# Two blocks of x turned by VectorE instead of TensorE in the projection stage of a fused attention and SwiGLU kernel

## The chip, the cores and the metric

The kernel runs on one core of a Trainium2 chip. The metric is the device time of one execution in microseconds (us); less is better. Three runs of the kernel before the change took 1405.27, 1405.49 and 1405.62 us, with a median of 1405.49 us.

## The reference

The input `x` has 2048 tokens of 512 features. It is layer-normalised, and the normalised `xn` goes two ways: into 32-head attention with heads of 16 features, and into a SwiGLU feed-forward of width 1792. The output is `x` plus the product of the two.

```python
def _A_ref(x, wqkv, wo):            # H = 32 heads, Dh = 16
    q, k, v = split(x @ wqkv)
    p = softmax(q @ k.T * Dh ** -0.5)
    return merge(p @ v) @ wo

def _B_ref(x, w_gate, w_up, w_down):
    return (silu(x @ w_gate) * (x @ w_up)) @ w_down

xn = _layernorm(x)
return x + _A_ref(xn, wqkv, wo) * silu(_B_ref(xn, w_gate, w_up, w_down))
```

## The kernel before

**Two stages.** The first stage, about 160 us of 1403 us, normalises `x`, turns it so that features lie on partitions, and makes q, k and v. They go to DRAM, together with the turned `x` (`xt_d`). The second stage runs attention and feeds the matmuls of the feed-forward into the same TensorE queue. The change touches the first stage only.

**Blocks and tiles.** The tokens are cut into NB = 4 blocks of TB = 512, and a block into NT = 4 pieces of 128 tokens. The loop `for b in range(NB)` makes twelve result tiles a block: in blocks 1 to 3 the tiles n = 0 to 7 are `feature_tile` (q and k, 128 features by 512 tokens) and n = 8 to 11 are `value_tile` (v, 128 tokens by 512 features). Every tile is one call of `project`: 12 matmuls, since each of the 4 slices of 128 features takes three products. Both the turned `x` and the weights are held as a high and a low part (`hi`, `lo`), and the products are high by high, low by high, high by low, in this order.

**What follows a tile.** After a feature tile ScalarE squares the result (`sq`, L701), casts it to the high part (`parts`, L702), VectorE subtracts to get the low part (L703), and the SP queue stores both (L705). After a value tile ScalarE copies it into `vt` (L719). The result banks `ps` are four. In block 0 and in the tiles 0 to 6 of block 1 ScalarE also copies a piece of the turned `x` of block 0 into `fx` (`copy_fx`, L732). At the end of tile 8 `flush(b)` puts the eight sums of squares on TensorE (`squares`, L663), each of which needs its `sq`, and VectorE takes two maxima (L743).

**How the next block is made.** While block b is projected, block b + 1 is prepared: the SP queue loads four pieces of `x` into `xin`, the tile `facc` under another name (`load_x`, L544); VectorE takes mean and variance of a piece (`stats`, L610 and L611); `rates` gets the inverse deviations, with a square root on ScalarE (L615 to L623); VectorE normalises (`norm`, L627); TensorE turns a piece by four transposes with an identity into a PSUM bank (`turn`, L631); and `split_x` makes the two parts, the high one by ScalarE (L636), the low one by VectorE (L639). After the last piece the POOL queue stores both parts (L645). The schedule by tile n is written out by hand:

```python
if n == (1 if b else 2) and more:
    load_x(b + 1)
...
if 2 <= n < 6:  stats(n - 2)
if n == 5:      rates(0, NT)
if 6 <= n < 10: norm(n - 6)
if 8 <= n < 11: turn_x(b + 1, n - 8)
if n == 10:     turn_x(b + 1, NT - 1)
```

The queues are in order: an instruction that waits holds up all behind it on its engine. The first matmul of the next block needs the high part of its first 128 features, and the second matmul the low part.

Of the kernel before, what the change touches and what calls it, by code (L numbers as in the profile page):

```python
# [9 lines left out]
F32 = mybir.dt.float32  # L10
# [3 lines left out]
AF = mybir.ActivationFunctionType  # L14
ALU = mybir.AluOpType
# [4 lines left out]
P = 128  # L20
# [6 lines left out]
TB = S // NB  # L27
NT = TB // P
DT = D // P
# [13 lines left out]
PROBS = 12  # L43
EPS = 1e-5
FINE = (30,)
QSLOT = (0, 1, 0)
KSLOT = (0, 0, 1)

# [2 lines left out]
def tile_block(ctx: ExitStack, tc: tile.TileContext, x, wqkv, wo, w_gate, w_up, w_down, out):  # L51
    nc = tc.nc
    ctx.enter_context(tc.manual_schedule())
    x, out = x[0], out[0]
    mm, act, dve, sp, pool = nc.tensor.matmul, nc.scalar.activation, nc.vector, nc.sync, nc.gpsimd
# [6 lines left out]
    xt_d = dram.tile([NB, 2, P, DT, TB], F32, name="xt_d")  # L62
# [31 lines left out]
    def load_rows(dst, src, slots):  # L94
        for h in range(2):
            for s, part in enumerate(slots):
                r = h * HALF + 2 + s * DH
                sp.dma_start(dst[r:r + DH].bitcast(F32),
                             src[part].rearrange("(j h d) t -> h d j t", j=2, h=2)[h])
# [5 lines left out]
    def load_q(u, i=None):  # L105
        g, b = divmod(u, NB)
        load_rows(qst[u % 2 if i is None else i], q_d[:, g * 64:(g + 1) * 64, b * TB:(b + 1) * TB], QSLOT)

# [382 lines left out]
    for u in range(units):  # L491
# [3 lines left out]
        elif u == 0:  # L495
            ns = [4, 6, 6]
        elif u in FINE:
            ns = [4] * 4
# [32 lines left out]
    with ExitStack() as pro:  # L531
        pc = pro.enter_context(tc.tile_pool(name="pc", bufs=1))
# [8 lines left out]
        xin = facc  # L541

        def load_tile(t):
            sp.dma_start(xin[:, t % NT], x[t * P:(t + 1) * P])  # L544

        def load_x(b):
            for t in range(NT):
                load_tile(b * NT + t)
# [50 lines left out]
        for t in range(NT):  # L599
            dve.memset(vt5[:, :, t, :, DH:], 1.0)  # L600
        xt = [[pc.tile([P, DT, TB], F32R, name=f"xt{i}{j}") for j in range(2)] for i in range(2)]
        mv = pc.tile([P, NT, dve.BN_AGGR_DIM], F32, name="mv")
        ve = pc.tile([P, NT], F32, name="ve")
        rs = pc.tile([P, NT], F32, name="rs")
        nw = pc.tile([P, NT], F32, name="nw")
# [2 lines left out]
        def stats(t):  # L608
            st = p2.tile([P, dve.BN_STATS_DIM], F32, tag="st", name="st")
            dve.bn_stats(st, xin[:, t])  # L610
            dve.bn_aggr(mv[:, t], st)  # L611

        def rates(first, last):
            r, n, v = (i[:, first:last] for i in (rs, nw, ve))
            dve.tensor_scalar(v, mv[:, first:last, 1], EPS, None, op0=ALU.add)  # L615
            act(n, v, AF.Sqrt)
            dve.reciprocal(r, n)
            each = [[i[:, t:t + 1] for i in (rs, nw, ve)] for t in range(first, last)]
            for rt, n1, vt1 in each:
                dve.tensor_scalar(n1, vt1, rt, rt, op0=ALU.mult, op1=ALU.mult)  # L620
            dve.tensor_scalar(n, n, -0.5, 1.5, op0=ALU.mult, op1=ALU.add)
            for rt, n1, _ in each:
                dve.tensor_scalar(rt, n1, rt, None, op0=ALU.mult)  # L623
# [10 lines left out]
        def split_x(b, t, av, between=None):  # L634
            hi, lo = (xt[b % 2][j][:, :, t * P:(t + 1) * P] for j in range(2))
            nc.scalar.copy(hi, av)  # L636
            if between:
                between()
            dve.tensor_sub(lo, av, hi.bitcast(F32))  # L639

        def turn_x(b, t, between=None):
            split_x(b, t, turn(t), between)
            if t == NT - 1 and b:
                for j in range(2):
                    pool.dma_start(xt_d[b, j], xt[b % 2][j].bitcast(F32))  # L645


        def project(pairs, xh, xl, tokens, order=None, ps=None):
# [21 lines left out]
        part = split_w(8, pool)  # L670
# [6 lines left out]
        part = split_w(10, pool)  # L677
# [67 lines left out]
        for b in range(NB):  # L745
            more = b + 1 < NB
            slots = [(feature_tile, m) for m in range(8)]
            slots = [(value_tile, t) for t in range(NT)] + slots if b == 0 else slots + [(value_tile, t) for t in range(NT)]
            for n, (make, i) in enumerate(slots):
                if b == 0:  # L750
                    if n + 5 < 12:
                        load_w(worder[n + 5])
                    if n >= 2 and n + 2 < 12:
                        split_w(worder[n + 2], pool)
                if n == (1 if b else 2) and more:
                    load_x(b + 1)
                if b == 2 and n in (6, 7):
                    load_gu(n - 6)
                if b == 2 and n == 8:
                    load_wd(0)  # L760
                if not more and n == 2:
                    split_gu(0)
                    tidy()
                    for bank in acc:
                        dve.memset(bank, 0.0)
                if not more and n in (1, 3):
                    load_k(0, n // 2)
                if not more and n == 5:
                    load_q(0)
                if not more and n == 6:  # L770
                    for c in range(2):
                        load_v(0, c)
                if b == 0 and n == 1:
                    rates(2, NT)
                    norm(2)
                    norm(3)
                    split_x(0, 0, xf)
                made = make(b, i)
                if b == 0 and n == 1:
                    for t in (2, 3):  # L780
                        turn_x(0, t)
                if b < 2 and 0 <= 12 * b + n - 3 < 16:
                    copy_fx(12 * b + n - 3)
                if n == 0 and b == 1:
                    flush(0)
                if make is feature_tile:
                    pend.append(made)
                if b == 0 and n == 11:
                    ring(0, 2, one)
                    queries(0, one)  # L790
                if more:
                    if 2 <= n < 6:
                        stats(n - 2)
                    if n == 5:
                        rates(0, NT)
                    if 6 <= n < 10:
                        norm(n - 6)
                    if 8 <= n < 11:
                        turn_x(b + 1, n - 8)
                    if n == 10:  # L800
                        turn_x(b + 1, NT - 1)
                if n == 8 and b:
                    flush(b)
                if not more and n == 8:
                    dve.reduce_max(pk, peak, axis=AX.X)
                    dve.tensor_add(sm, pk[:, 0:1], pk[:, 1:2])
                if not more and n == 9:
                    tops = pps.tile([P, 512], F32, tag="ps", name="tops")
                    nc.tensor.transpose(tops[0:1, :P], sm, ident)
                    dve.reduce_max(s4, tops[0:1, :P], axis=AX.X)  # L810
                    dve.tensor_scalar(s4, s4, 0.51, None, op0=ALU.mult)
                    dve.tensor_scalar(flag, s4, LIMIT, None, op0=ALU.is_le)
                    dve.tensor_scalar(sel[:, :NG * NB], row[:, :NG * NB], s4, None, op0=ALU.mult)
                    for h in range(2):
                        dve.tensor_copy(selq[:, h * HALF:h * HALF + 1], s4)
                    fill(3 * DC)
                    tidy()
                    low, high = [pps.tile([P, 512], F32, tag="ps", name="low") for _ in range(2)]
                    mm(high[:2 * NG * NB, :8], sel, row[:, :8], start=True, stop=True, skip_group_check=True)
                    mm(low[:HALF + 2, :8], selq, row[:, :8], start=True, stop=True, skip_group_check=True)  # L820
                    act(shift, high[:2 * NG * NB, 0:1].to_broadcast([2 * NG * NB, 512]), AF.Copy, scale=-1.0)
                    for h in range(2):
                        two_rows = slice(h * HALF, h * HALF + 2)
                        act(qst[0][two_rows], low[two_rows, None, 0:1].to_broadcast([2, 2, 512]), AF.Copy, scale=-1.0)
                    for j in range(4):
                        pool.dma_start(sh_d[:, j * 512:(j + 1) * 512], shift.bitcast(F32))
                    fast = nc.values_load(flag, min_val=0, max_val=1)


        with tc.If(fast < 1):  # L830
            with tc.tile_pool(name="gen", bufs=1) as gen:
                for h in range(2):
                    pool.memset(qst[0][h * HALF:h * HALF + 2].bitcast(F32), 0.0)
                for g in range(NG):
                    for b in range(NB):
# [3 lines left out]
                        for j in range(NB):  # L839
                            load_k(g, j, j % 2)  # L840
                            for i in range(4 * NT):
                                h, t = divmod(i, NT)
# [132 lines left out]
    for now, (u, first, n) in enumerate(blocks):  # L975
        g, b = divmod(u, NB)
# [25 lines left out]
    hi = two.tile([P, 2, D], F32R, tag="guh", name="rh")[:, 0]  # L1002
    lo = one.tile([P, D], F32R, tag="th", name="rl")
# [38 lines left out]
    part = low(1)  # L1042
# [35 lines left out]
```

## Time and profile before

| | before |
|---|---|
| median of 3 runs | 1405.49 us |
| the profiled execution | 1405.18 us |
| its span on the core | 1403.4 us |
| TensorE (PE) busy | 1395.8 us, 99% |
| ScalarE (ACT) busy | 1082.7 us, 77% |
| VectorE (DVE) busy | 753.5 us, 54% |
| GpSimd (POOL) busy | 90.6 us, 6% |
| granted TensorE clock, mean | 0.999 |

The profile is one execution. A row of the timeline gives the start in us from the start of the span, the duration, the engine, the line of the kernel, the operation, and in brackets the idle time of the engine ahead of it with what ended it. Instructions of one engine overlap at their ends, so that what counts in a queue is the distance from start to start. Tiles of the projection can be told by their `sq` (L701) and `vt` (L719) rows: one of these starts as each tile of TensorE ends.

### The profile page before, as it was taken

The page shows a single profiled execution, that of the slowest core. Times are in us where ns is not written, and L with a number is a line of the kernel's source. Part 1 is how long each engine was busy: PE and PEld are TensorE (multiplying, and loading weights), DVE is VectorE, ACT ScalarE, POOL GpSimd, SP SyncE. Part 2 cuts the span into 40 slices and gives each one's busy share as a digit, 9 for nine tenths or more (in the row PEclk, how much of TensorE's full clock was granted, in tenths as well). Part 3 has the DMA queues.
Part 4 walks back from the last instruction along what each step waited for, and adds up shares of the span by engine and source line. Part 5 has one row for each costly group of instructions (what it writes and reads, how often), then busy time and mean ns, then how long its engine had stood idle before and what let it go on. Part 6 is the DMA issues. An engine that isn't in the chain of part 4 may idle for free.

```text
span 1403.4 us, 27734 instructions
## 1 busy us (share of the span) xinstructions
PE 1395.8 (99%) x11227; PEld 847.1 (60%) x11227; DVE 753.5 (54%) x1291; ACT 1082.7 (77%) x1235; POOL 90.6 (6%) x104
## 2 busy tenths in 40 slices
PE   9999999999999999999999999999999999999998
PEld 7777756556555655565556556655655565565554
DVE  5544455345645553555456645654565446556655
ACT  6733587778788877887887788778877887888885
POOL 4200200000000000000000000000000000000333
PEclk9999999999999999999999999999999999999999
DMA  6768651033544521144524303256224113224333
GB/s 219 263 248 247 181 128 43 13 103 88 122 102 103 125 50 35 47 118 107 131 64 104 101 13 73 73 143 145 65 73 109 37 46 73 66 89 162 102 99 113
DMA packets 126956, 148.17 MB, mean 106 GB/s; under 512 B 12524, under 2 KB 79340, under 8 KB 126052
## 3 DMA queue, kind: packets, MB, share of 16 engines
q1 hardware_dynamic: 121620, 125.79, 34.2%
q0 software_dynamic: 4912, 20.12, 3.9%
q8 instruction: 91, 1.49, 0.4%
q14 instruction: 45, 0.37, 0.1%
q10 hardware_dynamic: 288, 0.39, 0.1%
HBM read 106.68 MB, written 39.58 MB: 104 GB/s over the span
## 4 chain that ended last, share of the span: by engine, by line
PE 88%; ACT 0%; DVE 0%; issue 0%; DVEq 0%; ACTq 0%
PE acc L406 32%; PE bankx L186 24%; PE score L888 17%; PE banky L186 12%; PE acc L888 3%; PE acc L1015 0%; PE banky L1015 0%; ACT pr L961 0%; ACT pr L894 0%; PE score L1015 0%; DVE y L1022 0%; DVE fx L280 0%; DVE part L300 0%; DVE y L191 0%; DVE pr L947 0%
## 5 line engine op out<-in xcount | busy, mean ns | idle before, releaser
L894 ACT ACTIVATE pr<-score 128x1024 f32<-128x1024 f32 x856 | 810.6, 1032 | 229.3 <-PE score L888 227.8
L406 PE MATMUL acc<-pr,vst 128*17 128x512 f32 x4096 | 461.9, 593 | 0.0
L888 PE MATMUL score<-qst,kst 50*128 50x512 f32 x1712 | 392.0, 413 | 0.0
L186 PE MATMUL bankx<-fx,guh 64*128 64x512 f32 x896 | 333.4, 393 | 0.1
L186 PE MATMUL banky<-fx,guh 64*128 64x512 f32 x896 | 324.5, 392 | 0.0
L406 PEld LDWEIGHTS acc<-pr,vst 128*17 128x17 f32 x4096 | 108.8, 97 | 286.4 <-issue 262.6
L888 PEld LDWEIGHTS score<-qst,kst 50*128 50x128 f32 x1712 | 176.0, 184 | 147.7 <-issue 67.2
L947 DVE COPY pr<-acc 128x512 f32<-128x512 f32 x168 | 116.2, 691 | 192.5 <-PE acc L888 187.0
L186 PE MATMUL bankx<-wd,hh 64*128 64x512 f32 x672 | 200.2, 392 | 0.0
L186 PE MATMUL banky<-wd,hh 64*128 64x512 f32 x672 | 197.8, 393 | 0.0
L186 PEld LDWEIGHTS bankx<-fx,guh 64*128 64x128 f32 x896 | 166.4, 186 | 18.0 <-issue 0.9
L186 PE MATMUL bankx<-fx,gul 64*128 64x512 f32 x448 | 175.4, 391 | 0.0
L186 PE MATMUL banky<-fx,gul 64*128 64x512 f32 x448 | 175.4, 391 | 0.0
L961 ACT ACTIVATE pr<-pr 128x1024 f32<-128x1024 f32 x168 | 172.5, 1079 | 0.0
L186 PEld LDWEIGHTS banky<-fx,guh 64*128 64x128 f32 x896 | 166.3, 186 | 6.1
L953 DVE COPY pr<-acc 128x512 f32<-128x512 f32 x168 | 116.2, 692 | 73.8 <-PE acc L888 60.3
L888 PE MATMUL acc<-qst,kst 50*128 50x512 f32 x336 | 135.4, 403 | 0.1
L239 DVE SCALAR_TENSOR_TENSOR ga<-th,bankx 128x512 f32<-128x512 f32 x56 | 38.5, 688 | 178.2 <-ACT th L238 178.2
L186 PEld LDWEIGHTS bankx<-wd,hh 64*128 64x128 f32 x672 | 124.9, 186 | 12.4
L186 PEld LDWEIGHTS banky<-wd,hh 64*128 64x128 f32 x672 | 124.4, 186 | 3.6
L186 PEld LDWEIGHTS bankx<-fx,gul 64*128 64x128 f32 x448 | 83.7, 187 | 10.3
L186 PEld LDWEIGHTS banky<-fx,gul 64*128 64x128 f32 x448 | 83.5, 186 | 3.6
(168 smaller groups left out, 1308.7 us busy)
## 6 DMA issues: line engine op xcount, KB each, us to landing
gur<-in_B_w_gate_dram SPq DMA_DIRECT2D x56, 256.0 KB
gur<-in_B_w_up_dram SPq DMA_DIRECT2D x56, 256.0 KB
wdr<-in_B_w_down_dram SPq DMA_DIRECT2D x56, 256.0 KB
kst<-k_d SPq DMA_DIRECT2D x192, 64.0 KB
qst<-q_d SPq DMA_DIRECT2D x192, 64.0 KB
fx<-xt_d SPq DMA_DIRECT2D x24, 512.0 KB
q_d<-parts SPq DMA_DIRECT2D x16, 512.0 KB
k_d<-parts SPq DMA_DIRECT2D x16, 512.0 KB
```

What stands on the lines that cost most here:

```text
L186: mm(banks[i], lhs[halves[i]], rhs[halves[i]], start=start, stop=stop)
L239: dve.scalar_tensor_tensor(ga, th, 1.0, bankx, op0=ALU.add, op1=ALU.mult)
L406: mm(acc[0][h * 32:h * 32 + DH + 1], v[:, kt % CT, h * (DH + 1):(h + 1) * (DH + 1)], probs[kt, h // 2][:, h % 2], start=kt == 0, stop=kt = ...
L888: mm(bank, k[r, j, kc * P:(kc + 1) * P], qst[u % 2][r, j], start=True, stop=True)
L894: act(pr, score[slot], AF.Exp, scale=0.25)
L947: dve.tensor_copy(probs[kt, j][:, 0], spare_bank)
L953: dve.tensor_copy(probs[kt, j][:, 1], spare_bank)
L961: act(probs[kt, j], probs[kt, j], AF.Exp, scale=0.25)
```

## The change

It concerns the preparation of the blocks 2 and 3, which runs during the blocks 1 and 2; block 1 is prepared during block 0 as before. The load is issued at tile 0 instead of tile 1. All statistics are taken at the tiles 2 and 3, and `rates` at tile 3. ScalarE normalises in place, by `Identity` with a scale and an offset for each partition (`norms`, at the tiles 3 and 4). Then VectorE turns the block by 16 transposes, each of 32 partitions by 512 elements, which writes 32 partitions of another tile, `xw`, in general in another quadrant (`turn_quarter`, from tile 5 on: 2, 2, 3, 3, 3, 3). Behind tile 10 `split_block` makes the parts, one 128-feature slice after the other: four ScalarE copies and four VectorE subtractions, and then the two stores. The 16 transposes of TensorE, the four `norm` of VectorE and the four `split_x` of each of these two blocks go away.

```diff
+TURNS = (0, 0, 0, 0, 0, 0, 2, 4, 7, 10, 13, 16, 16)
...
+        xw = pc.tile([P, DT, TB], F32, name="xw")
+        off = pc.tile([P, NT], F32, name="off")
...
             if t == NT - 1 and b:
-                for j in range(2):
-                    pool.dma_start(xt_d[b, j], xt[b % 2][j].bitcast(F32))
+                store_x(b)
+
+        def store_x(b):
+            for j in range(2):
+                pool.dma_start(xt_d[b, j], xt[b % 2][j].bitcast(F32))
+
+        def norms(first):
+            if first == 0:
+                dve.scalar_tensor_tensor(off, mv[:, :, 0], -1.0, rs, op0=ALU.mult, op1=ALU.mult)
+            for t in range(first, first + 2):
+                act(xin[:, t], xin[:, t], AF.Identity, scale=rs[:, t:t + 1], bias=off[:, t:t + 1])
+
+        quarter = [slice(i * 32, (i + 1) * 32) for i in range(4)]
+
+        def turn_quarter(i):
+            q, g = divmod(i, 4)
+            dve.transpose(xw[quarter[q]].rearrange("p c (t g l) -> p g t c l", g=4, l=32)[:, g],
+                          xin[quarter[g]].rearrange("p t (c q d) -> p q t c d", q=4, d=32)[:, q])
+
+        def split_block(b):
+            hi, lo = xt[b % 2]
+            for c in range(DT):
+                nc.scalar.copy(hi[:, c], xw[:, c])
+                dve.tensor_sub(lo[:, c], xw[:, c], hi[:, c].bitcast(F32))
+            store_x(b)
...
-                if n == (1 if b else 2) and more:
+                if n == (0 if b else 2) and more:
                     load_x(b + 1)
+                if more and b:
+                    for part in range(TURNS[n], TURNS[n + 1]):
+                        turn_quarter(part)
...
-                if more:
+                if more and b:
+                    if n in (2, 3):
+                        stats(2 * n - 4)
+                        stats(2 * n - 3)
+                    if n == 3:
+                        rates(0, NT)
+                    if n in (3, 4):
+                        norms(2 * n - 6)
+                    if n == 10:
+                        split_block(b + 1)
+                elif more:
                     if 2 <= n < 6:
                         stats(n - 2)
```

## The prediction

> **What bounds the kernel now.** I read the page's busy shares first, then the chain of work that ended last, then the first stage row by row.
>
> ```profile
> PE 1395.8 (99%) x11227; PEld 847.1 (60%) x11227; DVE 753.5 (54%) x1291; ACT 1082.7 (77%) x1235; POOL 90.6 (6%) x104
> PE 88%; ACT 0%; DVE 0%; issue 0%; DVEq 0%; ACTq 0%
> 82.00:84.00 2.00, 2.00 (x11) 1.61 (x10) 0.00 (x0) 0.59 (x1) 0.53 (x1) 1.00 0.79 328
> ```
>
> These are a line of the page's busy times, one of its chain, and a row of a table by stretches. TensorE (PE) is the chain, and the third row (a stretch across the border between blocks 1 and 2: PE, PEld, DVE, ACT and POOL busy, clock, DMA share, GB/s) shows it busy and at full clock there, with VectorE idle and ScalarE nearly so. So a TensorE instruction removed here is worth its time, if the next block's parts still come in time. What TensorE gives to the turns is read from the timeline, from the distances between the ends of tiles in blocks 1 and 2.
>
> ```profile
> 49.24 0.60 ACT L701 ACTIVATE sq<-ps 128x512 bf16<-128x512 f32 x1 [0.66 <-PE ps L656]
> 52.78 0.60 ACT L701 ACTIVATE sq<-ps 128x512 bf16<-128x512 f32 x1 [1.53 <-PE ps L656]
> 55.58 0.60 ACT L701 ACTIVATE sq<-ps 128x512 bf16<-128x512 f32 x1 [0.65 <-PE ps L656]
> ...
> 72.38 0.59 ACT L719 COPY vt<-ps 128x512 f32<-128x512 f32 x1 [1.72 <-PE ps L658]
> 83.22 0.59 ACT L719 COPY vt<-ps 128x512 f32<-128x512 f32 x1 [2.09 <-PE ps L658]
> ...
> 108.41 0.59 ACT L719 COPY vt<-ps 128x512 f32<-128x512 f32 x1 [1.72 <-PE ps L658]
> 119.26 0.59 ACT L719 COPY vt<-ps 128x512 f32<-128x512 f32 x1 [2.09 <-PE ps L658]
> ...
> 79.38 1.04 PE L631 MATMUL acc<-ident,xn 128*128 128x128 f32 x8
> ```
>
> A tile takes 55.58 − 52.78 = 2.80. With the eight sums of squares between, it takes 52.78 − 49.24 = 3.54, so these cost 0.74. From tile 8's end to tile 11's end lie three tiles, one set of squares and all 16 transposes: 83.22 − 72.38 = 10.84, less 3 × 2.80, less 0.74, leaves **1.70** for the transposes of block 1. Block 2 gives 10.85, so 1.71. Removed for good: **3.4 us**, 0.24% of the time. That is the most that the change can give.
>
> **What is put in its place, and when it ends.** Before, the pieces were normalised, turned and split one by one, so little was left at the end. Now the next block's first matmul needs ScalarE's copy of `xw`, which needs all 16 turns, and these need all four normalisations. That is one chain; it is added up from its start at tile 3.
>
> ```profile
> 58.38 0.60 ACT L701 ACTIVATE sq<-ps 128x512 bf16<-128x512 f32 x1 [0.79 <-PE ps L656]
> 58.88 0.58 ACT L702 CAST parts<-ps 128x512 fp32r<-128x512 f32 x1
> 59.48 1.05 ACT L732 CAST fx<-xt 64x1024 fp32r<-64x1024 f32 x1
> ...
> 59.49 0.69 DVE L703 TENSOR_TENSOR parts<-ps,parts 128x512 fp32r<-128x512 f32 x1 [0.85 <-ACT parts L702]
> 60.10 0.69 DVE L610 BATCH_NORM_STATS2 st<-facc 128x6 f32<-128x512 f32 x1
> 60.82 0.18 DVE L611 BATCH_NORM_AGGREGATE mv<-st 128x2 f32<-128x6 f32 x1
> 66.42 0.18 DVE L611 BATCH_NORM_AGGREGATE mv<-st 128x2 f32<-128x6 f32 x1
> 66.63 0.17 DVE L615 TENSOR_SCALAR ve<-mv 128x4 f32<-128x4 f32 x1
> 68.35 0.58 DVE L623 TENSOR_SCALAR rs<-nw,rs 128x1 f32<-128x1 f32 x4
> 95.49 0.18 DVE L611 BATCH_NORM_AGGREGATE mv<-st 128x2 f32<-128x6 f32 x1
> 95.59 0.67 DVE L703 TENSOR_TENSOR parts<-ps,parts 128x512 fp32r<-128x512 f32 x1
> ```
>
> *Statistics.* In block 1 tile 3's subtraction stands at 59.49 and two pieces follow: 0.61 to the first `stats`, 0.72 to its aggregate, 0.10 on, 0.72 again, 0.21 to `ve` at 61.85. From `ve` to the end of `rs` the trace shows 68.35 + 0.58 − 66.63 = 2.30, ScalarE's square root within it; `off` adds one small operation, 0.2 by the 0.17 of `ve`. So the factors are ready at 64.35. ScalarE's `norms` stand at the head of its queue and hold tile 4's `sq` (due at 58.38 + 2.80 = 61.2) behind them.
>
> ```profile
> 30.35 0.60 ACT L574 CAST wh<-wraw 128x512 fp32r<-128x512 f32 x1
> 30.86 0.59 ACT L701 ACTIVATE sq<-ps 128x512 bf16<-128x512 f32 x1
> L620 DVE TENSOR_SCALAR nw<-ve,rs 128x1 f32<-128x1 f32 x16 | 3.5, 268 | 0.2
> L615 DVE TENSOR_SCALAR ve<-mv 128x1 f32<-128x1 f32 x2 | 0.3, 154 | 0.1
> ```
>
> *Normalisations.* No row shows an `Identity` with a scale and an offset for each partition. The nearest are a ScalarE cast from SBUF, 0.60 long and 0.51 to the next, and on VectorE the price of two such operands, 268 − 154 ns = 0.11. I take 0.63 from start to start and 0.71 long; the ends are 0.51 and twice the surcharge, 0.74. The Trainium skill (ScalarE: Activation LUTs, What ACT_TABLE_LOAD costs) gives about 93 ns for each such operand of an activation. By that page the two would cost 0.19, an estimate, and the sum would be 0.6 higher; no run here shows it. In block 1: norms at 64.40 and 65.03; `sq` at 65.66, cast 66.16, `fx` copy 66.76; norms at 67.84 and 68.47, done at **69.2**. In block 2 there is no `fx` copy: on the old clock the cast of tile 3 (94.91, 0.58 long) lets the subtraction start at 95.52, so `ve` stands at 97.88, the factors at 100.38, norms at 100.43 and 101.06, `sq` 101.69, cast 102.19, norms at 102.79 and 103.42, done at **104.15**.
>
> ```profile
> 356.14 0.71 DVE L442 STREAM_TRANSPOSE o<-on 128x512 f32<-128x512 f32 x1
> 356.79 0.69 DVE L953 COPY pr<-acc 128x512 f32<-128x512 f32 x1
> ...
> 94.91 0.58 ACT L702 CAST parts<-ps 128x512 fp32r<-128x512 f32 x1
> L574 ACT CAST wh<-wraw 128x512 fp32r<-128x512 f32 x8 | 5.0, 620 | 0.1
> L417 DVE STREAM_TRANSPOSE o<-acc 128x512 f32<-128x512 f32 x31 | 22.2, 717 | 37.6 <-PE acc L406 37.6
> L426 DVE TENSOR_TENSOR on<-o,rl 128x256 f32<-128x256 f32 x31 | 12.9, 417 | 0.1
> 82.80 0.39 PE L658 MATMUL ps<-vl,xt 128*128 128x512 f32 x1
> 83.03 0.62 PE L656 MATMUL ps<-xt,wh 128*128 128x512 f32 x2
> 119.06 0.62 PE L656 MATMUL ps<-xt,wh 128*128 128x512 f32 x2
> ```
>
> *Turns.* These are rows of the timeline and of the groups by line. No row shows a turn of 32 partitions into another quadrant. The dense turn of as many elements per partition takes 0.71 and lets the next start after **0.65**; I take that, since the elements in each lane decide in all rows of this kind. Below, the bound is 0.61, the ordinary distance (59.49 to 60.10); above, 0.75, a turn from PSUM (717 ns) whose follower waits for its end. Sixteen turns are 10.4, and three subtractions and two maxima stand between them in VectorE's queue, 5 × 0.61 = 3.05: their own inputs come in time (tile 5's cast ends at 70.2, the subtraction's turn comes at 70.5). The last turn ends 0.05 after its distance: 69.2 + 13.5 = **82.7** and 104.15 + 13.5 = **117.65**. Then the copy 0.62 + 0.03 and the subtraction 0.69 + 0.03, as at the handovers in the rows: the second matmul of the next block at **84.1** and **119.05**.
>
> *Against before.* Its second matmul stood 0.62 − 0.39 = 0.23 behind the first, at 83.26 and 119.29. Block 1 is therefore 0.8 longer, block 2 0.2 shorter; the later slices follow at 0.6 each, faster than TensorE eats them (0.7 for three). Without a wait the matmuls would come 1.7 earlier, so TensorE stands 2.5 in block 1 and 1.5 in block 2. Sum: **+0.6**.
>
> *The rest is covered.* The eighth square of block 1 needs `sq` of tile 7. Behind the norms ScalarE still has tiles 5 and 6, with `sq`, cast and `fx` copy 2.2 each, so that this `sq` ends at 69.1 + 4.4 + 0.6 = 74.1. Tile 8 ends at 72.4 as before, and the squares would be through by 73.1; TensorE waits about 1.0, but the border's wait gets shorter by as much: it is part of the 2.5. Result banks come free in time: tile 9's needs the subtraction of tile 5, done at 71.2, and is wanted at 74. Not used any more on VectorE and ScalarE, `norm` and `split_x` lay beside matmuls and give nothing.
>
> ```profile
> 51.49 3.69 SPq L544 DMA_DIRECT2D facc<-in_A_x_dram  x4
> 57.72 0.69 DVE L610 BATCH_NORM_STATS2 st<-facc 128x6 f32<-128x512 f32 x1 [0.34 <-DMA facc<-in_A_x_dram]
> ```
>
> *The load.* Before, the first piece came 57.7 − 51.5 = 6.2 after its issue. In block 1 it now goes ahead of tile 0's store on SP, some 2.8 earlier, and lands near 55, the others up to 3.7 later; the first `stats` can start at 57.3 and the third at 60.1. In block 2 the load waits for the last turn (82.7) on SP with tile 0's store behind it; that store comes later than this anyway. The two POOL stores start later; nothing in this stage reads them. These are priced at nothing; a late piece would move the chain one for one.
>
> The profiled execution took 1405.18, 0.3 under the median of the runs. 1405.18 + 0.6 = 1405.8; against the median, **1406.1 us**. Differences within 0.2%, 2.8 us, count as no change, about what a measurement can tell here.
>
> **The rivals.** *The turns are dearer (slower).* Every hundredth of a microsecond on a turn costs 32 × 0.01 = 0.32. From 0.72 a turn the change is over 2.8 slower. At 0.85, an extra price for runs of 32 elements and the move between quadrants, it is 32 × 0.20 + 0.6 = +7.0: 1412.5. Against it speaks L426, whose runs of 16 take 417 ns for 256 elements, no more than dense work; for it, that nothing in the trace has 32 partitions or crosses. The Trainium skill (VectorE: DVE Perf Modes, Rules for kernel authors) advises TensorE for a 128×128 transpose when PSUM will do, and VectorE for 32×32 blocks; by engine time the rows agree, 10.4 here against 1.7. Chance 0.20; to 0.07 more I come by late loads and the dearer activation.
>
> *All is covered (faster).* If turns and normalisations leave no wait, the gain is 3.4: 1402.1. For it speaks VectorE's busy share of 54%; against it, that even at 0.55 a turn block 2 reaches its full 1.7, but block 1 still waits the 1.0 for the squares: −2.4, within 2.8. Chance 0.10.
>
> That the change does something else than it says I give nothing: the 32 transposes of TensorE are gone from its queue and 32 turns stand in VectorE's.
>
> **How the numbers follow.** The forecast case, turns of 0.61 to 0.72, holds 0.63. Its own range: 0.61 with activations at 0.51 is −1.3 − 1.0 + 0.6 = −1.7 (1403.8); 0.72 with 0.74 is 2.2 + 0.9 + 0.6 = +3.7 (1409.2). The range reaches down halfway towards the covered case, 1403.0, and up to turns near 0.78, 1410.2. Faster 0.10, same 0.63, slower 0.27.
>
> **What would show it.** Right: the rows of the turns at a distance near 0.65; the second matmul of blocks 2 and 3 waiting for VectorE's subtraction of `xt` from `xw`; TensorE idle by some 2.5 and 1.5 us before these borders, part of it in block 1 ahead of the squares; 3.4 us of transposes gone. Wrong: turns far from 0.65, `stats` waiting for the load, waits after 160 us that were not there, or no wait at the borders.

## The result, and the profile after

The changed kernel took 1412.47 us (median of 6 runs, 1411.14 to 1413.12) against 1405.34 us for the kernel before (6 runs, 1405.15 to 1405.62): a ratio of 1.005, with a 95% interval of 1.0037 to 1.0063. It is slower by about 7.1 us. The prediction said 1406.1 us with a range of 1403.0 to 1410.2; the result lies outside, on the slow side.

The profiled execution of the changed kernel took 1413.12 us with a span of 1411.3 us, 8.0 us more than the 1405.18 us and 1403.4 us of before. From its page come the busy times.

```profile
PE 1397.0 (99%) x11195; PEld 844.6 (60%) x11195; DVE 772.8 (55%) x1317; ACT 1088.9 (77%) x1243; POOL 89.5 (6%) x104
```

The 32 transposes are gone from TensorE (11227 to 11195 instructions), yet PE is busy for 1.2 us longer. So some of what remained on TensorE became slower, and the rest of the 8 us is idle time. The waits of TensorE between 40 and 165 us (line, awaited line, total us, times, longest us) name it. Behind the new code, line numbers are 26 higher: L682 and L684 are the matmuls of a tile, L689 the squares, L657 `norms`, L663 the turns, L669 and L670 the copy and the subtraction of `split_block`.

```profile
PE ps L682 <- ACT xt L669: 4.4, 2, 2.5
PE banky L689 <- ACT sq L727: 1.5, 1, 1.5
PE ps L682 <- DVE xt L670: 0.4, 2, 0.2
PE acc L634 <- DVE xt L642: 0.3, 1, 0.3
```

The first row is new: at both borders the first matmul waits for ScalarE's copy, and the third row is the second matmul waiting for the subtraction. The second row is the eighth square of block 1, waiting for `sq` of tile 7. The last row belongs to the end of block 0 and stands in the kernel before too, with the same 0.3. The table by stretches of 2 us (PE, PEld, DVE, ACT and POOL busy, clock, DMA share, GB/s) shows what the waits don't.

```profile
86.00:88.00 2.00, 2.00 (x7) 1.62 (x8) 1.70 (x3) 1.21 (x3) 0.54 (x2) 0.78 1.00 311
88.00:90.00 2.00, 2.00 (x6) 1.52 (x6) 0.00 (x0) 0.00 (x0) 1.43 (x2) 0.50 1.04 419
90.00:92.00 2.00, 2.00 (x9) 1.63 (x8) 0.69 (x1) 1.07 (x2) 0.00 (x0) 0.87 0.99 414
124.00:126.00 2.00, 1.48 (x3) 1.02 (x4) 1.71 (x3) 2.00 (x5) 0.00 (x0) 0.66 0.00 0
126.00:128.00 2.00, 2.00 (x6) 1.56 (x5) 0.79 (x2) 0.30 (x1) 1.46 (x3) 0.50 0.46 193
128.00:130.00 2.00, 2.00 (x10) 1.60 (x10) 0.00 (x0) 0.74 (x2) 0.51 (x1) 0.98 0.97 365
```

Before, the stretch across border 1 had a clock of 1.00 and eleven matmuls. Here the clock falls to half behind each border, and a busy stretch holds six. Clocks of 0.78, 0.50 and 0.87 over 2 us each make (0.22 + 0.50 + 0.13) × 2 / 0.5 = 3.4 us at half speed at border 1; 0.66, 0.50 and 0.98 make 3.4 us at border 2.

The timelines of TensorE and of ScalarE give the size of each part.

```profile
74.38 0.38 PE L689 MATMUL banky<-sq,ind 128*32 128x512 bf16 x1 [1.53 <-ACT sq L727]
82.93 0.40 PE L684 MATMUL ps<-vl,xt 128*128 128x512 f32 x1
85.22 0.50 PE L682 MATMUL ps<-xt,wh 128*128 128x512 f32 x1 [1.90 <-ACT xt L669]
85.95 0.50 PE L682 MATMUL ps<-xt,wh 128*128 128x512 f32 x1 [0.23 <-DVE xt L670]
121.39 0.40 PE L684 MATMUL ps<-vl,xt 128*128 128x512 f32 x1
124.31 0.51 PE L682 MATMUL ps<-xt,wh 128*128 128x512 f32 x1 [2.53 <-ACT xt L669]
125.04 0.79 PE L682 MATMUL ps<-xt,wh 128*128 128x512 f32 x1 [0.21 <-DVE xt L670]
```

```profile
90.09 0.60 ACT L727 ACTIVATE sq<-ps 128x512 bf16<-128x512 f32 x1 [2.88 <-PE ps L682]
93.15 0.60 ACT L727 ACTIVATE sq<-ps 128x512 bf16<-128x512 f32 x1 [1.98 <-PE ps L682]
129.26 0.60 ACT L727 ACTIVATE sq<-ps 128x512 bf16<-128x512 f32 x1 [2.96 <-PE ps L682]
167.21 0.59 ACT L745 COPY vt<-acc 128x512 f32<-128x512 f32 x1 [2.21 <-PE acc L684]
```

The rows of the kernel before that answer to these four of ScalarE, the first two tiles of block 2, the first of block 3 and the last of block 3:

```profile
86.02 0.60 ACT L701 ACTIVATE sq<-ps 128x512 bf16<-128x512 f32 x1 [2.21 <-PE ps L656]
88.82 0.60 ACT L701 ACTIVATE sq<-ps 128x512 bf16<-128x512 f32 x1 [1.73 <-PE ps L656]
122.05 0.60 ACT L701 ACTIVATE sq<-ps 128x512 bf16<-128x512 f32 x1 [2.21 <-PE ps L656]
160.08 0.59 ACT L719 COPY vt<-acc 128x512 f32<-128x512 f32 x1 [2.19 <-PE acc L658]
```

With the rows of the borders before, which the prediction shows, each point of the first stage can be compared (the last matmul of block 2 stood 0.23 ahead of 119.06):

| point | before | after | later by | what came in between |
|---|---|---|---|---|
| last matmul of block 1 | 82.80 | 82.93 | 0.13 | the wait for the square, some 1.8, less the transposes, 1.70 |
| second matmul of block 2 | 83.26 | 85.95 | 2.69 | border 1: 2.56 |
| end of the second tile of block 2 | 88.82 | 93.15 | 4.33 | half clock: 1.64 |
| last matmul of block 2 | 118.83 | 121.39 | 2.56 | the transposes, −1.77 |
| second matmul of block 3 | 119.29 | 125.04 | 5.75 | border 2: 3.19 |
| end of the first tile of block 3 | 122.05 | 129.26 | 7.21 | half clock: 1.46 |
| end of the last tile of block 3 | 160.08 | 167.21 | 7.13 | |

The 1.8 of the square are what the table leaves for it; its own row above shows 1.53 of idle time. So 1.8 + 2.56 + 3.19 = 7.6 us are waits, 1.64 + 1.46 = 3.1 us are the clock, and 3.5 us of transposes went. A further 0.8 of the 8.0 lies behind block 3, where the spans end 1244.1 (after) and 1243.3 us (before) later. It is there, at 0.7 to 1.0, in the six profiles below of kernels that turn blocks in this way, at 0.3 to 0.4 with four dense turns, at 2.5 with whole rows, and not with the load alone. Its cause was not found.

### The profile page after: what moved, and what is told of

Read it like the earlier page. It is cut to its first block, busy times and chain, and to the rows that moved or that the text cites. A ratio compares the mean times of both kernels' runs of the same rounds, so it can differ in the third digit from the quotient of the medians.

```text
span 1411.3 us, 27699 instructions
## 1 busy us (share of the span) xinstructions
PE 1397.0 (99%) x11195; PEld 844.6 (60%) x11195; DVE 772.8 (55%) x1317; ACT 1088.9 (77%) x1243; POOL 89.5 (6%) x104
## 3 DMA queue, kind: packets, MB, share of 16 engines
q8 instruction: 89, 1.46, 0.4%
## 4 chain that ended last, share of the span: by engine, by line
PE 87%; ACT 1%; DVE 0%; issue 0%; DVEq 0%; ACTq 0%
PE acc L407 32%; PE bankx L187 24%; PE score L927 17%; PE banky L187 10%; PE acc L927 3%; ACT pr L933 0%; PE acc L1054 0%; PE banky L1054 0%; ACT pr L1000 0%; PE score L1054 0%; DVE pr L986 0%; DVE y L1061 0%; DVE fx L281 0%; DVE y L192 0%; DVE part L301 0%
## 5 line engine op out<-in xcount | busy, mean ns | idle before, releaser
L682 PE MATMUL ps<-xt,wh 128*128 128x512 f32 x256 | 83.6, 407 | 4.9 <-ACT xt L669 4.4
```

The source lines that it names most:

```text
L682: mm(ps, w, a[:, c], start=n == 0, stop=n == 3 * DT - 1)
```

## The experiments

### Does the chain of turns make the waits?

Four dense turns take the place of sixteen, all at tile 5, so that the chain ends long before the border. The moves between quadrants (groups of 32 partitions) are left out, so the blocks are not wholly turned; everything else stays.

```diff
-TURNS = (0, 0, 0, 0, 0, 0, 2, 4, 7, 10, 13, 16, 16)
+TURNS = (0, 0, 0, 0, 0, 0, 4, 4, 4, 4, 4, 4, 4)
-            dve.transpose(xw[quarter[q]].rearrange(...)[:, g], xin[quarter[g]].rearrange(...)[:, q])
+            dve.transpose(xw[:, :, i * P:(i + 1) * P], xin[:, i].rearrange("p (c f) -> p c f", c=DT))
```

> Four turns of 128 partitions, one for each piece of 128 tokens, stand at tile 5 in place of the 16 turns of 32 partitions; the moves between quadrants are left out, so what is computed downstream of xw is not the reference. Theory (the chain of 16 turns ends too late): twelve turns of 0.72 less are 8.6 us less chain in each block, so the waits of 2.6 and 3.2 us at the borders and the half clock behind them (1.6 and 1.5 us) go; what stays is the wait of 1.7 us for the squares in block 1. Time 1405.3 - 3.4 + 1.7 = 1403.6, and the clock stays at 1.00 at the borders. Rival (the time is lost to something that the change moves elsewhere: the load, the shifted buffers, the stores of the turned x): the time stays near 1412. The distance of these dense turns tells whether 0.72 instead of 0.65 belongs to turns of 32 partitions (then 0.65 here) or to any turn that follows a turn (0.72 here).

Measured: 1404.15 us (10 runs, 1403.5 to 1405.76) against 1405.18; ratio 0.9994 (0.9985 to 1.0004). All waits of TensorE in the same stretch, of this kernel:

```profile
PE banky L687 <- ACT sq L725: 1.4, 1, 1.4
PE acc L634 <- DVE xt L642: 0.3, 1, 0.3
```

The waits at the borders are gone, and with them the loss of clock (the mean granted clock is 1.000). The wait of the square, which comes from `norms` on ScalarE, stays. So everything at the borders comes from the end of the turns. From the end of block 0 (the row of its last `sq`, 46.44 before) to the end of block 3 (160.08) this kernel's profile is 1.8 shorter than before (111.82 us against 113.64): the transposes' 3.4, less some 1.6 for the square.

### Is the half clock a cost of the waits?

The changed kernel, with matmuls into an unused bank in the idle time at the borders, eight at the first and ten at the second.

```diff
+                    if n == 11:
+                        for _ in range((0, 8, 10)[b]):
+                            mm(acc[0], wh[:, 0, 0], vh[:, 0], start=True, stop=True)
```

> The changed kernel, with 8 and 10 matmuls of 512 columns more behind tile 11 of blocks 1 and 2, into a PSUM bank that nobody reads. They take 0.23 us each, 1.9 and 2.3 us, and end before the copy that the next block waits for (waits of 2.05 and 2.68 us to the first matmul). Theory (the TensorE clock halves because TensorE stands idle at the border): the clock stays at 1.00 and the 3.1 us of slow matmuls go, 1412.5 - 3.1 = 1409.4; the waits themselves stay. Rival (the matmuls behind the border are slow because of the parts that are written and stored at the same time): they stay slow, 1412.5 or more.

Measured: 1409.92 us (1409.77 to 1410.62); ratio 1.0036 (1.0022 to 1.0049). The stretches that stood at 0.50:

```profile
88.00:90.00 2.00, 2.00 (x11) 1.60 (x10) 0.36 (x1) 1.07 (x2) 1.14 (x2) 1.00 1.02 365
126.00:128.00 2.00, 2.00 (x11) 1.61 (x10) 0.69 (x1) 1.08 (x2) 0.67 (x1) 1.00 1.01 389
```

Eleven matmuls a stretch at full clock, and 1412.47 − 1409.92 = 2.55 less in the medians (1413.12 − 1409.92 = 3.2 between the profiled executions, where the table above has 3.1). Matmuls that nobody uses make the changed kernel faster, since the clock stays up; the subtractions that end the waits come no earlier by them (38.7 us behind the end of block 0 at border 1, with and without).

### Does one border's wait lose the clock more readily?

Only four such matmuls at each border (`range(4)`).

> The changed kernel, with only 4 matmuls more behind tile 11 of blocks 1 and 2 (8 and 10 took the half clock away). They leave TensorE idle for about 1.1 us and 1.75 us to the first matmul of the next block, where it was 2.05 and 2.68, and 0.5 more to the second. If the clock halves by the length of the idle time and the bound lies near 2 us, both borders keep the clock at 1.00 and the time is that of the kernel with 8 and 10, 1409.9. If any wait of over 1 us does it, the clock halves at both and the time stays at 1412.5. If the bound lies between, only block 2 shows it: about 1411.4.

Measured: 1411.58 us (1410.37 to 1412.43); ratio 1.0042 (1.0028 to 1.0056). Its profile has 2.5 of waiting for the copies at the borders in all, 1.56 at border 2 and 0.98 at border 1.

```profile
PE ps L682 <- ACT xt L669: 2.5, 2, 1.6
```

```profile
88.00:90.00 2.00, 2.00 (x10) 1.60 (x9) 0.28 (x1) 0.60 (x2) 1.57 (x3) 1.00 0.92 329
126.00:128.00 2.00, 2.00 (x7) 1.52 (x6) 0.00 (x0) 0.00 (x0) 1.43 (x2) 0.50 0.95 389
```

The wait of 0.98 kept the clock, that of 1.56 lost it, in this execution. Of the five, one of 1410.37 us has a mean clock of 1.000, where this one, of 1412.43, has 0.998, so border 2 seems not to lose it each time.

### The load alone

The kernel before, with only its load put where the change has it.

```diff
-                if n == (1 if b else 2) and more:
+                if n == (0 if b else 2) and more:
                     load_x(b + 1)
```

> The kernel before, with one edit: the load of the next block is issued at tile 0 instead of tile 1 in blocks 1 and 2. Theory: nothing that TensorE waits for hangs on the load, 1405.3 and within 0.2 us. Rival (the moved load holds up the stores of q and k on its queue and through them the later start): up to 0.8 us slower, the part of the loss that lies behind 160 us.

Measured: 1405.36 us (10 runs) against 1405.18; ratio 1.0002 (0.9992 to 1.0011). The times show no cost, and can't tell one below 1.5 us; the profile has no wait in the first stage that was not there before.

### The change for block 3 alone

Block 2 is prepared as before; only block 3, prepared in block 2, is turned by VectorE (`if b == 2` at the schedule and at the turns, load at `n == (2, 1, 0, 0)[b]`).

> The change made for block 3 alone: block 2 is prepared as before the change. Theory: the two borders add up one by one. This one removes 1.7 us of transposes, adds 3.2 of waiting and 1.5 of half clock: 1405.2 + 3.0 = 1408.2, with no wait for the squares, since in block 2 ScalarE has no copies to fx. Rival (the wait of block 3 is handed on from block 2, whose late border shifts the whole preparation): no wait at this border, 1403.5 to 1404.

Measured: 1409.6 us (7 runs, 1407.48 to 1410.56); ratio 1.003 (1.0019 to 1.0042). The wait is there, so block 3's slowness is not something that block 2's brings along. But the profiled execution, of 1407.63 us, kept its clock:

```profile
PE ps L682 <- ACT xt L669: 2.5, 1, 2.5
```

```profile
122.00:124.00 2.00, 2.00 (x10) 1.64 (x9) 0.66 (x2) 0.39 (x2) 1.57 (x3) 1.00 0.47 197
```

The seven runs have mean granted clocks of 1.000 at 1407.48 and 1407.63, 0.998 at 1408.91 and 1409.6, and 0.997 at 1410.41, 1410.5 and 1410.56. The time follows the clock. The short ones show what the change costs for block 3 without any loss of clock; the longest take some 3 us more, about twice what one stretch at half clock cost in the changed kernel (1.64 and 1.46). So one such stretch at this border can't be all of it.

The same kernel with ten matmuls in the idle time (those of the second experiment, behind tile 11 of block 2) should then be short every time:

> The change for block 3 alone, with 10 matmuls more behind tile 11 of block 2, which leave TensorE idle for 0.4 us instead of 2.5. The kernel without them spread over 3.1 us, 1407.48 to 1410.56, and its profiled execution, a short one of 1407.63, kept the clock at 1.00 behind the wait. Theory (whether the clock halves behind a wait of this length differs from execution to execution, and this is the spread): all executions come near the short ones, 1407.5, within 0.6 us of each other. Rival (the spread has another cause, the loads or stores at the border): it stays at some 3 us.

Measured: 1407.65 us (10 runs, 1407.27 to 1408.1); ratio 1.0016 (1.0006 to 1.0025). The spread shrinks from 3.1 to 0.8, and the long executions are gone. But these ten ran on another chip than the seven, and of the kernel without the matmuls only the next one ran there. A second profile of the kernel without them was taken to catch a long execution:

> The change for block 3 alone once more, for a second profile of the same kernel. Theory: if this execution takes about 1410.5, the clock behind the border is 0.5 for some 3 us; if it takes about 1407.6, it is 1.00. Rival: a long execution at full clock, or a short one at the half.

It took 1407.56 us: a wait of 2.5 again, and the clock at 1.00 again. That a long execution of this kernel loses its clock at this border is supported by its runs' mean clocks and by the steady executions with the matmuls, but no profile shows it, nor where the rest of the 3 us goes.

Why did a wait of 2.5 keep the clock here, where 1.56 lost it? The traces suggest that its place decides. In the changed kernel's trace the clock changes at 87.10, 90.52, 124.65 and 128.06 us, and once more behind the last matmul, at 1411.47: the steps between are 1, 10, 1 and 376 times 3.413 us. Counted back in such steps from the one drop of the clock in this kernel's first profile, at 1406.27, a boundary falls at 119.44, into the wait, which lasts from 117.69 to 120.18. These are the stretches ahead of the two drops of the changed kernel, and then the two that hold the wait of this one:

```profile
83.69:87.10 3.41, 1.65 (x6) 1.16 (x7) 2.71 (x6) 2.55 (x5) 0.07 (x1) 1.00 0.46 134
121.24:124.65 3.41, 0.88 (x4) 0.29 (x2) 2.68 (x5) 1.01 (x2) 0.00 (x0) 1.00 0.22 84
```

```profile
116.03:119.44 3.41, 1.66 (x8) 1.00 (x6) 3.35 (x5) 0.00 (x0) 0.00 (x0) 1.00 0.58 212
119.44:122.85 3.41, 2.44 (x9) 1.80 (x10) 2.54 (x5) 2.67 (x5) 0.54 (x1) 1.00 0.00 0
```

TensorE was idle for 1.76 and 2.53 us of the stretches ahead of the drops, and for 1.78 with four matmuls; here the idle time is divided into 1.75 and 0.97, and the clock stays. This is an explanation and not shown: 1.75 and 1.76 are too close to give a bound, in the last kernel below a stretch near its end, from 1395.03 to 1398.44, has 1.83 of idle time and keeps the clock, and no run moved a wait against the boundaries.

### What a turn's price hangs on

Each turn now takes 32 partitions and one whole row of 512 elements; it stays in its quadrant in block 1 and goes to the next one in block 2.

```diff
-            dve.transpose(xw[quarter[q]].rearrange(...)[:, g], xin[quarter[g]].rearrange(...)[:, q])
+            dve.transpose(xw[quarter[(q + b - 1) % 4], g], xin[quarter[q], g])
```

> The changed kernel with other access patterns in its 16 turns: each turns 32 partitions of one whole row of 512 elements into one whole row, in block 1 within its own quadrant, in block 2 into the next one; the order of the elements in xw is therefore not the reference's. Dense turns of 128 partitions stood 0.68 apart (2.73 for four, 0.70 for the last), the kernel's own 0.72. If the runs of 32 elements make the difference, 0.68 here in both blocks; if the 32 partitions do, 0.72 in both; if the move between quadrants does, 0.68 in block 1 and 0.72 in block 2.

Measured: 1407.72 us in one execution. The last six turns of both blocks, of this kernel:

```profile
79.25 3.80 DVE L663 STREAM_TRANSPOSE xw<-facc 32x512 f32<-32x512 f32 x6
114.70 3.80 DVE L663 STREAM_TRANSPOSE xw<-facc 32x512 f32<-32x512 f32 x6
```

two groups of three turns ahead of the first of these, of this kernel:

```profile
73.28 1.89 DVE L663 STREAM_TRANSPOSE xw<-facc 32x512 f32<-32x512 f32 x3
75.93 2.01 DVE L663 STREAM_TRANSPOSE xw<-facc 32x512 f32<-32x512 f32 x3
```

and of the changed kernel (rows of VectorE):

```profile
69.55 1.41 DVE L663 STREAM_TRANSPOSE xw<-facc 32x512 f32<-32x512 f32 x2 [1.93 <-ACT facc L657]
70.99 0.69 DVE L729 TENSOR_TENSOR parts<-ps,parts 128x512 fp32r<-128x512 f32 x1
71.71 1.42 DVE L663 STREAM_TRANSPOSE xw<-facc 32x512 f32<-32x512 f32 x2
73.88 2.13 DVE L663 STREAM_TRANSPOSE xw<-facc 32x512 f32<-32x512 f32 x3
80.22 4.30 DVE L663 STREAM_TRANSPOSE xw<-facc 32x512 f32<-32x512 f32 x6
108.63 1.41 DVE L663 STREAM_TRANSPOSE xw<-facc 32x512 f32<-32x512 f32 x2 [0.73 <-ACT facc L657]
119.31 4.30 DVE L663 STREAM_TRANSPOSE xw<-facc 32x512 f32<-32x512 f32 x6
```

On average the six turns stand (4.30 − 0.70) / 5 = 0.72 apart in the change and (3.80 − 0.70) / 5 = 0.62 with whole rows, in both blocks; 0.70 is about the length of one turn. So neither the 32 partitions nor the move into another quadrant raises the price of a turn. But the experiment changes one thing more. In the changed kernel each turn reads another quadrant than the one before it (quadrant i mod 4 for turn i, counted from 0); here four turns in a row read one quadrant and write one. The groups of three tell the two apart. The three at 73.28 all stay in one quadrant and take 1.89. Those at 75.93 change it once, after their first turn, and take 2.01, with the same whole rows. The three of the change at 73.88 change it twice, and take 2.13. So each change of the quadrant from one turn to the next costs 0.12, and nothing is left for the runs of 32 elements by which a turn of the change gathers its input and scatters its output: the six at 79.25 change once, those at 80.22 five times, and 4 × 0.12 is their difference of 0.50 but for 0.02. A price of such runs that this wait hides is not excluded, since no turn of the change follows one of its own quadrants.

The dense turns of the first experiment, which write runs of 128 elements, agree. Their two groups:

```profile
68.37 2.73 DVE L662 STREAM_TRANSPOSE xw<-facc 128x512 f32<-128x512 f32 x4
104.44 2.48 DVE L662 STREAM_TRANSPOSE xw<-facc 128x512 f32<-128x512 f32 x4
```

In block 2 they stand (2.48 − 0.67) / 3 = 0.60 apart. In block 1 the last two wait for ScalarE's third and fourth normalisation, which end only at about 69.64 and 70.35 there, so that 2.73 gives no price.

### Two tiles earlier

If the end of the chain is all that costs, the whole chain has to start earlier. The load goes to tile 10 of the block before, and each step moves ahead by one to two tiles.

```diff
-TURNS = (0, 0, 0, 0, 0, 0, 2, 4, 7, 10, 13, 16, 16)
+TURNS = (0, 0, 0, 0, 2, 4, 6, 8, 11, 14, 16, 16, 16)
-                if n == (0 if b else 2) and more:
-                    load_x(b + 1)
+                if b == 0 and n == 2:
+                    load_x(1)
+                if b < 2 and n == 10:
+                    load_x(b + 2)
...
-                    if n in (2, 3):
+                    if n in (0, 1):
...
-                    if n in (3, 4):
+                    if n in (1, 2):
```

> The changed kernel with its preparation two tiles earlier: the load at tile 10 of the block before, statistics at tiles 0 and 1, the normalisations at tiles 1 and 2, the turns from tile 3 on (2, 2, 2, 2, 3, 3, 2), the split still behind tile 10. Theory: the last turn then ends 5.6 us earlier, more than the waits of 2.6 and 3.2 us, so both border waits and the half clock go; the squares of block 1 wait less than 1.7 us, as ScalarE has two tiles more to catch up. Time 1402.0 with no wait left, 1403.5 with the whole wait for the squares. Rival (the work on VectorE slows others down, or the load comes late and the statistics wait for it): 1405 or more.

Measured: 1403.24 us (11 runs, 1402.95 to 1404.24) against 1405.18; ratio 0.9987 (0.9978 to 0.9996). This is 1.9 us faster than the kernel before. Its waits of TensorE, and the end of its chain on VectorE:

```profile
PE acc L634 <- DVE xt L642: 0.3, 1, 0.3
PE banky L689 <- ACT sq L727: 0.2, 1, 0.2
```

```profile
78.88 1.43 DVE L663 STREAM_TRANSPOSE xw<-facc 32x512 f32<-32x512 f32 x2
80.99 2.49 DVE L670 TENSOR_TENSOR xt<-xw,xt 128x512 fp32r<-128x512 f32 x4 [0.69 <-ACT xt L669]
```

The same turns at the same 0.72 now end at 80.3 instead of 84.5. The first subtraction ends at 81.7, the first matmul comes at 81.84, and nothing waits at the borders. From the end of block 0 to the end of block 3 it is 2.9 shorter than before (110.71 against 113.64 us); 0.9 of that is given back behind block 3, the open part named above.

## Why the prediction was wrong

**What held.** The mechanism was the predicted one: the transposes left TensorE, the chain from `norms` over sixteen turns to copy and subtraction set the border, and TensorE stood before both borders and before the square in block 1. The load was priced at nothing, and the experiment with the load alone saw no cost. The slow rival stood on the right step, "the turns are dearer", with 0.72 a turn as the point from which it decides. They came out at just that point, which by itself is 32 × 0.07 = 2.2 more than forecast, though not for the runs of 32 elements that the rival names beside the move between quadrants. Two other durations were too small as well, and one effect had no term.

**The turns, 0.65 against 0.72.** The sentence that failed is "the elements in each lane decide in all rows of this kind". Where a turn stays in the quadrants of the one before it, it stands 0.60 to 0.62 behind it; where it leaves them, it starts only when that one has ended, 0.70 long, which makes 0.72. In the change every turn leaves those of the turn before it. No line that the prediction took its price from shows such a change. L426, with its runs of 16, was a fair witness: no price of the runs shows here.

**What stands between the turns, 0.61 against 0.72.** The prediction put the three subtractions and two maxima at the ordinary distance. Next to a turn in another quadrant it doesn't hold: subtraction and turn are 71.71 − 70.99 = 0.72 apart. (Where the turn starts in the subtraction's own quadrant, as in the first experiment, it is 68.37 − 67.76 = 0.61.) Together with the turns, the stretch from the first turn to the end of the last is 80.22 + 4.30 − 69.55 = 14.97 in block 1, where 13.5 was expected: 1.5 too small in each block, 1.05 of it from the turns and 0.4 from what stands between.

**The normalisations.** From the groups by line of the changed kernel, and ScalarE's timeline:

```profile
L657 ACT ACTIVATE facc<-facc,off,rs x8: 799/810/819, 64.4 to 107.8; 128x512 f32<-128x512 f32 x8
```

```profile
64.42 1.52 ACT L657 ACTIVATE facc<-facc,off,rs 128x512 f32<-128x512 f32 x2 [2.12 <-DVE off L655]
```

One takes 0.81, the next follows after 0.71; predicted were 0.71 and 0.63. They start at 64.42 (predicted 64.40) and the turns at 69.55 (69.2). The 0.81 is 0.21 over a plain copy's 0.60, for two operands; the trace had only VectorE's 0.11 for two to offer. The Trainium skill's 93 ns for each such operand (ScalarE: Activation LUTs, What ACT_TABLE_LOAD costs) makes 0.19 and was nearer. By that page the prediction's sum would have been 0.6 higher.

These three put the second matmul of block 2 at 85.95 instead of 84.1: 1.85 late. At border 2, the 4.33 by which block 2 already runs late set aside, it is 1.66 late. The square's wait became some 1.8 instead of 1.0; as predicted, the border's wait is shorter by as much, so that it doesn't add to the sum.

**The clock, which was missing altogether.** The prediction quoted a clock of 1.00 across the border and never asked what an idle TensorE does to it. It costs 3.1, and the matmuls at the borders take it back. The predicted +0.6, plus 1.85 and 1.66 for the late chain, plus 3.1, makes 7.2; 7.13 was measured. Without the loss of clock the result would have been just inside the range, as the median of 1409.92 with the matmuls is. The range was built of durations alone, and had nothing for the speed of the matmuls behind a wait.

## What to carry to other kernels

When work leaves the engine that bounds a kernel, work out when its replacement ends, and price a wait by its length and by what the clock does behind it. A chain on an idle engine is free only if it starts early enough: the same turns lost 7 us when they began at tile 5, and won 2 when the whole chain stood two tiles ahead. Take an operation's price from a row whose neighbour stands to it as it will in the new kernel, in the same quadrant or in another, and where no such row is there, make the range as wide as that could cost.

## What the runs showed of the hardware

- A wait of TensorE of 1.6 to 2.5 us can halve its clock for 3.4 us behind it, at some 1.5 us apiece. The length alone doesn't decide: 1.6 (border 2, with four matmuls), 1.90 and 2.53 (the change) lost the clock, while 2.5 kept it in two profiles of the change for block 3 alone, as 1.4 and 1.5 at the squares did. The clock changes at whole multiples of 3.413 us from one another, and how much of a wait falls between two such points may decide; that is not shown. The Trainium skill (TensorE: Matmul & The Clock Gate, What's actually happening) describes a window of about 3.4 us that runs freely; the clock is halved after an idle window and restored after a busy one. The 3.4 us at half speed and the difference between executions agree with it. That a whole window of idleness is needed does not: 1.6 us sufficed.
- A transpose by VectorE of 512 elements for each partition takes 0.70 and lets the next start after 0.60 to 0.62, with 32 partitions and runs of 512 as with 128 partitions and runs of 128. A move into another quadrant within one transpose costs nothing.
- When successive instructions of VectorE change the quadrant, the next starts only when the one before has ended: 0.72 from start to start instead of some 0.61, between two turns and between a turn and a subtraction.
